# A room of 768 KB for the SyncE transfers of a gated-scan attention and FFN kernel

## The chip, the core and the metric

One core of a Trainium2 chip runs the whole kernel in one launch. The metric is the device time of that launch in microseconds (us), taken over several runs. The core has five engines with a queue of their own each: TensorE (PE; its weight loads are PEld), VectorE (DVE), ScalarE (ACT), GpSimd (POOL) and SyncE (SP). SP does no arithmetic here: it issues nearly all the transfers (DMAs), one after the other in the order in which the program wrote them. POOL issues the rest.

## The reference

```python
def _attn_ref(q, k, v, a_re, a_im):          # each (4, 8, 768, 48)
    mag = np.sqrt(a_re * a_re + a_im * a_im)
    scale = np.minimum(mag, 0.999) / (mag + 1e-06)
    a_re_n, a_im_n = (a_re * scale, a_im * scale)
    for t in range(S):
        ar, ai = (a_re_n[:, :, t, :, None], a_im_n[:, :, t, :, None])
        new_re = ar * S_re - ai * S_im
        new_im = ar * S_im + ai * S_re
        kv = np.einsum('bhd,bhe->bhde', k[:, :, t], v[:, :, t])
        S_re, S_im = (new_re + kv, new_im)
        y[:, :, t] = np.einsum('bhd,bhde->bhe', q[:, :, t], S_re)
    return y

def _moe_ref(x, w1, w2, w3, w_out):          # x is (3072, 384): y with its heads beside each other
    a = x @ w1                               # w1, w2: (384, 1024)
    b = x @ w2
    h = a * b @ w3                           # w3: (1024, 1024)
    return h @ w_out                         # w_out: (1024, 384)
```

## The kernel before, in words

**Units.** The 4 batches of 768 time steps are cut into 8 units of 384 steps (`u` = 0 to 7, two to a batch; `TT` = 384), and a unit into three chunks of 128. For each unit, DVE and ACT turn the gates `a_re` and `a_im` into running products of magnitude and running sums of angle and multiply them into `q` and `k` (`gates`, L574, a generator of some thirty steps). SP moves the results from one layout of the on-chip memory to another as the tiles `KL` and `QL` (12 transfers a unit, `move`, L733). PE then transposes (`turn`, "tr"), builds the state (`state`, "kv"), the scores (`scores`, "sc", which read `KL` and `QL`) and the outputs (`outputs`, "y"), and ACT copies the outputs to `xT` (L815). The FFN of a unit runs on PE while the next unit's attention is fed in between: `ffn_ab` (L844) makes `a * b` (products at L852, ACT copies one at L857, DVE multiplies at L859), `ffn_out` and `out_pair` multiply by the product of `w3` and `w_out`, which was made once at the start (`fuse`, L1140).

**Weights.** `w1` and `w2` arrive as 64-bit words and are rounded to 32 bits on DVE and ACT, in four blocks of 256 columns, `n` = 0 to 3 (`w12_ops`, L1108, and `weight_ops`, L980: DVE at L992, L1006 and L1009, ACT at L997). `fetch` (L962) loads a block: one transfer for the part of `w1` and one for that of `w2`, 768 KB each, into one `raw` tile. There are two `raw` tiles, so block 2 may be loaded when block 0 is rounded, block 3 when block 1 is.

**The order on SP.** From the start of the planned part on (`paced` is filled there) the program order is SP's order. Around the change it is: the rest of block 0; V of unit 0 (`turn_v`, 14 transfers of 18 to 72 KB); block 1; block 2; V of unit 1; block 3; `k`, `q` (three transfers of 192 KB each) and `vr` (576 KB) of unit 1; `re` and `im` of unit 2; the moves of unit 1; outputs. Later units repeat: V, `re`, `im`, the 12 moves, `k`, `q`, outputs and `vr`. `im` of unit u+1 goes into the buffer that unit u's cosine used, so it waits for DVE's L719; `re` waits for the end of the angle sums (L687, L690).

**What SP waits for already.** A transfer waits for the buffer that it fills and for the data that it reads. Each transfer uses one of eight completion counters in turn, so it waits too for the transfer eight places before it. Two single holds are written by hand: the part of `w2` of block 1 waits for the DVE copy of unit 0's second half of the scores of chunk 1 (`pending`, `behind`, L532), and `k`, `q` and `vr` of unit 4 (`LATER`) are issued only at the end of unit 3, behind ACT's last copy of its outputs.

**The planner.** `run` (L1268) decides on the host, with a simple clock, between which PE pieces the gate steps are written; for the first pieces a fixed `PLAN` does. Beside that, POOL reads every weight and part of the gates once more and tests their range (`check_weights`, the tile `look`, 256 KB at a time by its own DMA queue).

Of the kernel before, what the change touches and what calls it, by code (L numbers as in the profile page):

```python
# [376 lines left out]
def kernel(  # L377
# [36 lines left out]
    nc = tc.nc  # L414
    B, H, D, S = qt.shape
    P = 128
# [16 lines left out]
    LO, HI = 32, D - 32  # L433
    PASS, WIDE, SCAN, LAND, SLACK, LATE, RING, LOOK, NEAR, EARLY = 1.17, 1.4, 1.05, 1.8, 0.7, 1.2, 8, 4.0, 4, 2
    LOOKS = 3
    LATER = (4,)
    PLAN = ("- uc c cu c uu - cu uu cuuuc - - cc - - uc uu u - uuucu ucuu u u cuccc uccuucuu - - uu uucc uuc u "
            "uuucu cc ccc ccc cc ccc - - - c - - - - - - c - - c c c cc - cc - ccc - c - cc cc - cc ccc ccc - c c "
            "cccc - - - o - - ").split()
# [53 lines left out]
    st_ang = singles.tile([P, NU, KD, UC], FP, name="st_ang")  # L493

    g_t, L_t, xT_t, ab_t, T_t, KT_t = {}, {}, {}, {}, {}, {}

    clock = dict(PE=0.0, ACT=0.0, DVE=0.0, POOL=0.0, SP=0.0, DMA=0.0)
    ready, landings = {}, [0.0] * RING
# [7 lines left out]
            landings.append(clock["DMA"])  # L506
        ready[name] = clock["DMA"] + 0.2

    def load_rows(dst, src, u, which=range(KD), queue=nc.sync, key=None):
        b, h = divmod(u, 2)  # L510
        for i, f in enumerate(which):
            ins = queue.dma_start(out=dst[:, i, 0:TT], in_=src[b, :, DG * f:DG * (f + 1), h * TT:(h + 1) * TT].rearrange(  # L512
                "h d s -> d h s"))
            if key and i == 0:
                behind(ins, key)

    def load_gates(u, names=("re", "im"), after=()):
        g = g_t.setdefault(u, {})
# [8 lines left out]
        g["q"] = gate_pool[u % 2].tile([P, KD, TT], FP, tag="q", name="q")  # L527
        g["k"] = gate_pool[u % 2].tile([P, KD, TT + 1], FP, tag="k", name="k")

    last = {}  # L530

    def behind(ins, key):  # L532
        if key in last:
            tc.add_manual_dep(ins.ins, last[key].ins.name, BEHIND, reason="room")

    def load_qkv(u, key=None):
        b, h = divmod(u, 2)
        if "q" not in g_t.get(u, {}):
            take_qk(u)
        g = g_t[u]  # L540
        load_rows(g["k"], kt, u, key=key)
        load_rows(g["q"], qt, u)
        landed(("q", u))

    def load_v(u):
        b, h = divmod(u, 2)


        vr = one.tile([P, UC, DM], FP, tag="vr", name="vr")
        nc.sync.dma_start(out=vr, in_=v[b, h * TT:(h + 1) * TT].rearrange("(c p) e -> p c e", p=C))  # L550
        g_t[u]["vr"] = vr

    def turn_v(u):
        b, h = divmod(u, 2)
        src = v[b, h * TT:(h + 1) * TT].rearrange("(c p) (h d) -> p c h d", p=C, d=D)
        for hd in range(H):
            r = SB * (hd % LANES)
            for p0, p1, s0 in ((r, C, 0), (0, r, C - r)):
                if p1 > p0:
                    nc.sync.dma_start(out=Vb[u % 2][p0:p1, :, hd, 0:D], in_=src[s0:s0 + p1 - p0, :, hd])  # L560

    def check_gates(u, re, junk, x):
        scale, bias = ((-1.0, LEAST), (1.0, MOST))[x]
        nc.scalar.activation(out=junk, in_=re, func=AF.Relu, scale=scale, bias=bias, accum_out=st_low[:, x, u, 0:1])

    chained, paced = [], []

    def chain(ins):

# [4 lines left out]
    def gates(u, split):  # L574
# [158 lines left out]
        def move(dst, src, s):  # L733
            for x in range(2):
                for f in range(KD)[s]:
                    nc.sync.dma_start(out=dst[x * KD + f::2 * KD], in_=src[x][:, f])

        for s in [slice(f, f + 1) for f in range(KD)] if split else parts:
            if split:
# [5 lines left out]
                tt(out=q[:, s], in0=q[:, s], in1=Z[:, s], op=OP.mult)  # L745
            move(QL, (A, q), s)
        landed("moves", ("ks", "qs"), 4 * KD, 0.95)
        if 2 < u + 1 < NU and u + 1 not in LATER:
            load_qkv(u + 1)
        yield None  # L750

# [19 lines left out]
    def scores(u, c, x):  # L771
        QL, KL = L_t[u][0:2]
        w = slice(c * C, (c + 1) * C)
        A = Ab[(u * UC + c) % 2]
        n = H // 2
        sc = Sc[x]
        for s0 in SPANS:
            for j in range(n):
                g = (s0 // SB + j) % LANES
                nc.tensor.matmul(out=sc[SB * g:SB * g + SB, j, s0:C], lhsT=KL[:, x * n + j, w][:, s0:s0 + SB],  # L780
                                 rhs=QL[:, x * n + j, w][:, s0:C], start=True, stop=True)
        with tc.high_priority():
            last["sc", u, c, x] = nc.vector.copy_predicated(out=A[:, x * n:(x + 1) * n], data=sc, mask=mask)  # L783


    SPANS = (0, 3 * SB, SB, 2 * SB)
# [7 lines left out]
    def outputs(u, c):  # L794
        QL = L_t[u][0]
        w = slice(c * C, (c + 1) * C)
        A, V = Ab[(u * UC + c) % 2], Vb[u % 2][:, c]
        if c == 0:
            xT_t[u] = two.tile([P, KD, TT], FP, tag="xT", name="xT")
        T = T_t.get((u // 2, u % 2 * UC + c))  # L800
        first = T is None
        y = ps_v.tile([P, KD, C], FP, tag="v", name="y")
        lanes = [[] for _ in range(4)]
        for i, q in enumerate(QUADS):
            f, j = divmod(i, 4)
            o = y[32 * j:32 * j + 32, f]
            got = [(part(V, hd, e), A[:, hd]) for hd, e in q]
            if not first:
                got += [(part(T, hd, e), QL[:, hd, w]) for hd, e in q]
            lanes[j] += [(o, a, b, n == 0, n == len(got) - 1) for n, (a, b) in enumerate(got)]  # L810
        for step in zip(*lanes):
            for o, a, b, s0, s1 in step:
                nc.tensor.matmul(out=o, lhsT=a, rhs=b, start=s0, stop=s1)  # L813
        with tc.high_priority():
            last["y", u, c] = nc.scalar.copy(out=xT_t[u][:, :, w], in_=y)  # L815

    Tb = [singles.tile([2 * D, H, 64], FP, name=f"T{i}") for i in range(3)]
    for T in Tb:
# [2 lines left out]
    def state(u, c):  # L821

        KT, V = KT_t.pop((u, c)), g_t[u]["vr"][:, c].rearrange("p (h d) -> p h d", d=D)
        n = u % 2 * UC + c
        T = T_t.get((u // 2, n))
        kv = ps_v.tile([2 * D, H, D], FP, tag="v", name="kv")
        for hd in range(H):
            rows = KT[:, hd].rearrange("p d x f -> p (d x f)")
            for g in range(0, 2 * D, SB):
                nc.tensor.matmul(out=kv[g:g + SB, hd], lhsT=rows[:, g:g + SB], rhs=V[:, hd], start=True, stop=True)  # L830
        Tn = Tb[(u * UC + c) % 3]
        with tc.high_priority():
            if T is None:
                nc.scalar.copy(out=Tn[:, :, 0:D], in_=kv)
            else:
                nc.vector.tensor_tensor(out=Tn[:, :, 0:D], in0=kv, in1=T[:, :, 0:D], op=OP.add)
        if c == UC - 1:
            rho = L_t[u][1][:, :, TT:TT + 1].to_broadcast([2 * D, H, D])
            nc.vector.tensor_tensor(out=Tn[:, :, 0:D], in0=Tn[:, :, 0:D], in1=rho, op=OP.mult)
        T_t[u // 2, n + 1] = Tn  # L840
        if 1 < u + 1 < NU and u + 1 not in LATER and c == UC - 1 - u % 2:
            load_v(u + 1)

    def ffn_ab(u, j):  # L844
# [40 lines left out]
    def out_pair(u):  # L885
# [5 lines left out]
        def done(t, half):  # L891
            r0 = u * TT + t * P
            if u == NU - 1:
                s = slice(half * DH, (half + 1) * DH)
            elif half == 0:
                return
            else:
                s = slice(0, DM)
            nc.sync.dma_start(out=out[r0:r0 + P, s], in_=o[t][:, s])

        def product(p, bank, i):
            if i == 0:
# [32 lines left out]
    def ffn_out(u, t, parts=1):  # L935
        got = {}

        def part(f0):
            if f0 == 0:
                got["m"] = ps_m.tile([P, DM], FP, tag="mm", name="o")  # L940
            m = got["m"]
            for f in range(f0, f0 + KF // parts):
                nc.tensor.matmul(out=m, lhsT=ab_t[u][:, f, t * P:(t + 1) * P], rhs=w3o[:, f],  # L943
                                 start=(f == 0), stop=(f == KF - 1))
            if f == KF - 1:
                o = (late[0] if u else two).tile([P, DM], FP, tag="o", name="ot")
                nc.scalar.copy(out=o, in_=m)
                r0 = u * TT + t * P
                nc.sync.dma_start(out=out[r0:r0 + P, :], in_=o)
        return [lambda i=i: part(i * KF // parts) for i in range(parts)]  # L950


# [4 lines left out]

    cv = {}

    pending = []  # L960

    def fetch(srcs, early=None, wait=None):  # L962

        if srcs[0].dtype == FP:
            return srcs
# [3 lines left out]
        for src in srcs:  # L969
            r, m = src.shape[1:]  # L970
            t = raw[:, n:n + r * m].rearrange("p (r m) -> p r m", r=r)
            if wait and got:
                pending.append(lambda t=t, src=src: behind(nc.sync.dma_start(out=t, in_=src), wait))
            else:
                nc.sync.dma_start(out=t, in_=src)
            got.append(t.rearrange("p r (m w) -> p r m w", w=2))
            n += r * m
# [100 lines left out]
    def columns(src, j0, j1):  # L1078
        n = 1 if src.dtype == FP else 2
        return words(src)[:, :, n * j0:n * j1]  # L1080
# [3 lines left out]
    def w12_load(n, parts=slice(0, KD), early=()):  # L1084
# [9 lines left out]
                got.setdefault(n, []).append((parts, k, raw.rearrange("p r (m w) -> p r m w", w=2)))  # L1094
        if not early:
            got.setdefault(n, []).extend((parts, k, t) for k, t in enumerate(
                fetch([columns(w, n * WB, (n + 1) * WB)[:, parts] for w in (w1, w2)],
                      wait=("sc", 0, 1, 1) if n == 1 else None)))
        landed(("raw", n), (), 2, 2.2)

    def w12_early():
# [166 lines left out]
    def run(seq):  # L1268
# [82 lines left out]
        for k, (kind, f) in enumerate(seq):  # L1351
# [11 lines left out]
                held.update(tr=[], kv=0)  # L1363
            elif kind == "end":
                ended[0] = f
                if f + 1 in LATER:
                    load_qkv(f + 1, ("y", f, UC - 1))
                    load_v(f + 1)
                if f == 1:
                    load_qkv(2)  # L1370
                    turn_v(2)
# [7 lines left out]
            else:  # L1379
                if kind == "sc":  # L1380
                    clock["PE"] = max(clock["PE"], ready["moves"])
                if kind == "y0" and pending:
                    pending.pop()()
                item(kind)
                f()
                if k >= len(PLAN):
# [114 lines left out]
```

## Time and profile before

| | us |
|---|---|
| runs | 549.95, 549.74, 546.41 (median 549.74) |
| the profiled execution | 552.84 |
| its span, first to last instruction | 551.0 |
| PE busy in the span | 519.4 |
| POOL busy / DVE busy | 361.6 / 359.9 |
| SP's DMA queue busy | 48.1% of the 16 engines' span |

All transfers land on 16 DMA engines. The median times from issue to landing, with the size of one transfer, from the page's last part:

```profile
look<-in_w_dram POOLq DMA_DIRECT2D x56, 256.0 KB, 3.8
...
KL<-gR SPq DMA_DIRECT2D x24, 192.5 KB, 5.3
KL<-k SPq DMA_DIRECT2D x24, 192.5 KB, 6.0
...
k<-in_k_dram SPq DMA_DIRECT2D x24, 192.0 KB, 7.6
q<-in_q_dram SPq DMA_DIRECT2D x24, 192.0 KB, 7.3
...
raw<-in_w_dram SPq DMA_DIRECT2D x6, 768.0 KB, 5.1
```

How to read the lines that follow in this document. A timeline line holds the start, the busy time, the engine, the line of the program, the operation, what it writes and reads, how often, and in brackets how long its engine sat idle before it and what ended that. A line of SP says when a transfer was issued, not when it landed; times of landing are from the trace's record of each transfer's completion. A line of windows holds the stretch, its length, the busy time of PE, PEld, DVE, ACT and POOL, the clock granted to PE (1.00 is full), the share of the DMA engines' time, and GB/s.

### The profile page before, as it was taken

The numbers are of one execution on the slowest core, as the hardware profiler recorded it, in microseconds if no ns is written. First come the engines' busy times: TensorE is split into PE (matmuls) and PEld (weight loads), VectorE is DVE, ScalarE is ACT, GpSimd is POOL, SyncE is SP. The second block draws the span as 40 slices with busy tenths as digits, with TensorE's granted clock in tenths as the row PEclk, the third lists the DMA queues.
The fourth block names the chain that finished last, engine by engine and source line by source line (L and its number), as shares of the span: only waits on it lengthen the run. The fifth ranks groups of instructions, "written<-read, shape, count | busy, mean of one in ns | idle before, by whom it ended". The sixth has DMA issues, their size and how long they took to land.

```text
span 551.0 us, 13249 instructions
## 1 busy us (share of the span) xinstructions
PE 519.4 (94%) x5474; PEld 357.7 (65%) x5474; DVE 359.9 (65%) x520; ACT 273.7 (50%) x391; POOL 361.6 (66%) x425
## 2 busy tenths in 40 slices
PE   4789799989999999999998999999999999999995
PEld 2345475547656885669664875678567956696574
DVE  7999598856586669675956788597448851331131
ACT  6988866636544464754374626934276323101100
POOL 1000000488888888888998899899899988888000
PEclk9899999999999999999999999999999999999998
DMA  8999677594669835592889348933792182223001
GB/s 269 358 404 271 159 238 186 167 213 139 158 171 225 230 98 152 130 216 67 230 191 239 112 123 181 228 104 115 172 243 81 56 225 67 74 81 87 0 3 49
DMA packets 73222, 89.73 MB, mean 163 GB/s; under 512 B 31808, under 2 KB 62976, under 8 KB 72384
## 3 DMA queue, kind: packets, MB, share of 16 engines
q1 hardware_dynamic: 67072, 69.78, 48.1%
q0 software_dynamic: 6080, 19.01, 12.1%
q8 instruction: 45, 0.74, 0.6%
q14 instruction: 25, 0.20, 0.1%
HBM read 65.14 MB, written 4.72 MB: 127 GB/s over the span
## 4 chain that ended last, share of the span: by engine, by line
PE 74%; DVE 7%; DMA 7%; ACT 4%; SPq 4%; issue 3%; DVEq 0%; ACTq 0%
PE m L852 34%; PE p L907 12%; PE o L943 9%; PE y L813 6%; PE sc L780 5%; DMA im<-in_a_im_dram 3%; PE kv L830 3%; PE f L1145 2%; SPq L512 2%; PE tp L766 2%; DMA raw<-in_w_dram 1%; DMA q<-in_q_dram 1%; PE sc L1145 1%; ACT gZ L586 1%; DMA out_dram<-ot 1%
## 5 line engine op out<-in xcount | busy, mean ns | idle before, releaser
L852 PE MATMUL m<-xT,w1s 128*128 128x384 f32 x384 | 134.8, 487 | 1.2 <-ACT xT L815 1.2
L852 PE MATMUL m<-xT,w2s 128*128 128x384 f32 x384 | 135.1, 488 | 0.0
L852 PEld LDWEIGHTS m<-xT,w1s 128*128 128x128 f32 x384 | 72.2, 190 | 48.9 <-ACT xT L815 1.7
L852 PEld LDWEIGHTS m<-xT,w2s 128*128 128x128 f32 x384 | 71.5, 190 | 46.2
L1064 POOL TENSOR_SCALAR look<-look 128x256 f32<-128x256 f32 (+1 forms) x84 | 88.3, 1052 | 7.3
L859 DVE TENSOR_TENSOR ab<-m,a 128x384 f32<-128x384 f32 x64 | 35.2, 553 | 72.1 <-PE m L852 67.1
L1045 POOL TENSOR_TENSOR seen<-seen,look 128x256 bf16<-128x256 bf16 (+1 forms) x84 | 77.1, 918 | 6.8
L857 ACT COPY a<-m 128x384 f32<-128x384 f32 x64 | 30.2, 472 | 100.8 <-PE m L852 100.8
L1029 POOL MEMSET seen<- 128x256 bf16 x1 | 0.3, 311 | 98.9 <-DVE w2s L1009 98.9
L943 PE MATMUL o<-w3o,ab 128*128 128x384 f32 x160 | 54.3, 489 | 2.3 <-DVE ab L859 2.3
L1061 POOL TENSOR_TENSOR look<-look 128x256 f32<-128x256 f32 (+1 forms) x72 | 52.8, 733 | 3.0 <-DMA look<-in_w_dram 1.2
L1063 POOL TENSOR_SCALAR look<-look 128x256 f32<-128x256 f32 (+1 forms) x44 | 48.4, 1101 | 4.9 <-DMA look<-in_a_re_dram 1.7
L1066 POOL TENSOR_TENSOR look<-look 128x256 f32<-128x256 f32 (+1 forms) x44 | 42.9, 975 | 3.7
L1040 POOL DMA_DIRECT2D look<-in_w_dram x56 | 33.1, 591 | 16.6 <-POOL seen L1045 16.6
L943 PEld LDWEIGHTS o<-w3o,ab 128*128 128x128 f32 x160 | 29.7, 190 | 21.9 <-DVE ab L859 2.9
L783 DVE COPY_PREDICATED A<-mask,sc 128x512 f32<-128x512 uint8 x48 | 32.7, 734 | 12.9 <-PE sc L780 12.9
L813 PE MATMUL y<-A,V 128*32 128x128 f32 x768 | 39.4, 273 | 0.0
L768 ACT COPY KT<-tp 128x384 f32<-128x384 f32 x40 | 34.2, 863 | 6.4 <-PE tp L766 6.4
L813 PE MATMUL y<-QL,T 96*32 96x128 f32 x640 | 34.9, 272 | 0.8 <-issue 0.8
L813 PEld LDWEIGHTS y<-A,V 128*32 128x32 f32 x768 | 34.2, 110 | 1.6 <-issue 1.6
L815 ACT COPY xT<-y 128x384 f32<-128x384 f32 x24 | 11.4, 476 | 47.4 <-PE y L813 47.4
L1145 PE MATMUL f<-wo_s,w3s 128*128 128x384 f32 x96 | 34.6, 509 | 0.0
(123 smaller groups left out, 892.8 us busy)
## 6 DMA issues: line engine op xcount, KB each, us to landing
look<-in_w_dram POOLq DMA_DIRECT2D x56, 256.0 KB, 3.8
raw<-in_w_dram SPq DMA_DIRECT2D x6, 1024.0 KB, 10.3
KL<-gR SPq DMA_DIRECT2D x24, 192.5 KB, 5.3
KL<-k SPq DMA_DIRECT2D x24, 192.5 KB, 6.0
re<-in_a_re_dram SPq DMA_DIRECT2D x24, 192.0 KB, 3.9
im<-in_a_im_dram SPq DMA_DIRECT2D x24, 192.0 KB, 4.3
k<-in_k_dram SPq DMA_DIRECT2D x24, 192.0 KB, 7.6
q<-in_q_dram SPq DMA_DIRECT2D x24, 192.0 KB, 7.3
```

Of the source, the lines that this page charges most:

```text
L768: nc.scalar.copy(out=KT_t[u, c][:, :, :, x].rearrange("p h d f -> p f d h"), in_=tp.rearrange("p f (d h) -> p f d h", h=H))
L813: nc.tensor.matmul(out=o, lhsT=a, rhs=b, start=s0, stop=s1)
L852: nc.tensor.matmul(out=m, lhsT=w[:, j * P // WB, f, j * P % WB:j * P % WB + P], rhs=xT_t[u][:, f], start=(f == 0), stop=(f == KD - 1))
L859: nc.vector.tensor_tensor(out=ab_t[u][:, j], in0=m, in1=got[0], op=OP.mult)
L907: nc.tensor.matmul(out=m[p], lhsT=a[:, f], rhs=b[:, f], start=(f == 0), stop=(f == KH - 1))
L943: nc.tensor.matmul(out=m, lhsT=ab_t[u][:, f, t * P:(t + 1) * P], rhs=w3o[:, f], start=(f == 0), stop=(f == KF - 1))
L1045: nc.gpsimd.tensor_tensor(out=seen[:, 0:n], in0=seen[:, 0:n], in1=x, op=OP.add)
L1061: tt(out=x, in0=x, in1=x, op=OP.mult)
L1063: ts(out=y, in0=x, scalar1=high, scalar2=None, op0=OP.is_le)
L1064: ts(out=x, in0=x, scalar1=low, scalar2=None, op0=OP.is_ge)
L1066: tt(out=x, in0=x, in1=y, op=OP.mult)
L1145: nc.tensor.matmul(out=sums[j], lhsT=w3_t[f][:, j * P:(j + 1) * P], rhs=w3_t["wo"][:, f], start=(f == 0), stop=(f == KF - 1))
```

## The change

A list `flights` keeps the size of every transfer that SP issues from the planned part on. A new transfer adds up sizes backwards, itself first; at the first older transfer with which the sum passes `ROOM` (768 KB), it is made to wait until that one has landed. `w1` and `w2` go out by row (256 KB, three to a part), so that they fit. Both single holds go; `k`, `q` and `vr` of unit 4 then take the place that they have in the other units. All of SP's transfers of the planned part go through `transfer`; POOL's do not.

```diff
-    LATER = (4,)
+    ROOM = 4 * 192 * 1024
...
+    paced, flights = [], []
+
+    def transfer(dst, src):
+
+        ins = nc.sync.dma_start(out=dst, in_=src)
+        if paced:
+            size = total = 4 * math.prod(dst.shape)
+            for other, n in reversed(flights):
+                total += n
+                if total > ROOM:
+                    tc.add_manual_dep(ins.ins, other.ins.name, BEHIND, reason="room")
+                    break
+            flights.append((ins, size))
...
-    def load_rows(dst, src, u, which=range(KD), queue=nc.sync, key=None):
+    def load_rows(dst, src, u):
         b, h = divmod(u, 2)
-        for i, f in enumerate(which):
-            ins = queue.dma_start(out=dst[:, i, 0:TT], in_=src[b, :, DG * f:DG * (f + 1), h * TT:(h + 1) * TT].rearrange(
-                "h d s -> d h s"))
-            if key and i == 0:
-                behind(ins, key)
+        for f in range(KD):
+            transfer(dst[:, f, 0:TT], src[b, :, DG * f:DG * (f + 1), h * TT:(h + 1) * TT].rearrange("h d s -> d h s"))
...
-                    nc.sync.dma_start(out=Vb[u % 2][p0:p1, :, hd, 0:D], in_=src[s0:s0 + p1 - p0, :, hd])
+                    transfer(Vb[u % 2][p0:p1, :, hd, 0:D], src[s0:s0 + p1 - p0, :, hd])
...
-                    nc.sync.dma_start(out=dst[x * KD + f::2 * KD], in_=src[x][:, f])
+                    transfer(dst[x * KD + f::2 * KD], src[x][:, f])
...
-        if 2 < u + 1 < NU and u + 1 not in LATER:
+        if 2 < u + 1 < NU:
             load_qkv(u + 1)
...
-            if wait and got:
-                pending.append(lambda t=t, src=src: behind(nc.sync.dma_start(out=t, in_=src), wait))
-            else:
+            for i in range(r) if paced else ():
+                transfer(t[:, i], src[:, i])
+            if not paced:
                 nc.sync.dma_start(out=t, in_=src)
...
-                if f + 1 in LATER:
-                    load_qkv(f + 1, ("y", f, UC - 1))
-                    load_v(f + 1)
...
-                if kind == "y0" and pending:
-                    pending.pop()()
```

The loads of `vr` and the stores of the outputs call `transfer` in the same way.

## The prediction

> **What bounds the kernel now.** I read the page first, then the windows, then the timelines of PE, DVE and SP around PE's waits. The page's busy line and its chain:
>
> ```profile
> PE 519.4 (94%) x5474; PEld 357.7 (65%) x5474; DVE 359.9 (65%) x520; ACT 273.7 (50%) x391; POOL 361.6 (66%) x425
> ...
> PE 74%; DVE 7%; DMA 7%; ACT 4%; SPq 4%; issue 3%; DVEq 0%; ACTq 0%
> ```
>
> TensorE works through nearly the whole span, so only what opens or closes one of its gaps counts. The windows (start:end, length, busy time of each engine, granted clock, DMA share, GB/s) show where gaps are left; PE is full from 80 to 100 and is not in the other two rows:
>
> ```profile
> 80.00:100.00 20.00, 20.00 (x64) 11.79 (x63) 17.76 (x27) 12.71 (x15) 0.00 (x0) 1.00 0.81 229
> 100.00:120.00 20.00, 17.70 (x62) 10.50 (x61) 15.03 (x15) 11.26 (x17) 14.89 (x18) 1.00 0.64 164
> ...
> 280.00:300.00 20.00, 17.29 (x152) 10.85 (x151) 10.59 (x13) 13.53 (x17) 17.73 (x20) 1.00 1.02 219
> ```
>
> Of the time in which the change acts (from 69 us on), PE lacks 2.3 us before 120, 2.7 at 294, 1.06 at 245 and some 1.4 around 140. PE's timeline names the first:
>
> ```profile
> 117.55 0.91 PE L943 MATMUL o<-w3o,ab 128*128 128x384 f32 x2 [2.30 <-DVE ab L859]
> ```
>
> VectorE's timeline shows why that product came late:
>
> ```profile
> 94.33 0.56 DVE L992 TENSOR_SCALAR low<-raw 128x768 int32<-128x768 int32 x1 [1.62 <-DMA raw<-in_w_dram]
> ...
> 99.58 1.38 DVE L654 TENSOR_TENSOR k<-k,gR 128x1152 f32<-128x1152 f32 x1
> ...
> 102.19 1.37 DVE L656 TENSOR_TENSOR q<-q,gA 128x1152 f32<-128x1152 f32 x1
> ...
> 115.58 1.46 DVE L600 TENSOR_TENSOR im<-im,gR 128x1152 f32<-128x1152 f32 x1 [1.64 <-DMA im<-in_a_im_dram]
> 116.95 0.54 DVE L859 TENSOR_TENSOR ab<-m,a 128x384 f32<-128x384 f32 x1
> ```
>
> DVE waits for weight block 3 at 94.33, then runs unit 1's gate steps (k, q, then L702, ACT's cosine, L717, L719). L719 frees the buffer into which SP loads unit 2's `im`; L600 waits for that, and the product that PE needs stands behind L600. From 94.33 to 117.55 there is no slack. SP's timeline shows what feeds it:
>
> ```profile
> 69.24 0.41 SPq L975 DMA_DIRECT2D raw<-in_w_dram  x1
> 73.83 0.38 SPq L973 DMA_DIRECT2D raw<-in_w_dram  x1
> 76.72 0.90 SPq L975 DMA_DIRECT2D raw<-in_w_dram  x2
> 77.67 11.27 SPq L560 DMA_DIRECT2D V<-in_v_dram  x14
> 89.05 0.93 SPq L975 DMA_DIRECT2D raw<-in_w_dram  x2
> 90.03 1.96 SPq L512 DMA_DIRECT2D k<-in_k_dram  x3
> 92.03 2.05 SPq L512 DMA_DIRECT2D q<-in_q_dram  x3
> ```
>
> Block 1 (first two lines, the second held), block 2, V of unit 1, block 3, then k and q of unit 1, in one queue.
>
> **The change, part by part.** PE, DVE, ACT and POOL keep their instructions and order; only SP's list differs. On SP, 6 transfers of 768 KB become 18 of 256 KB, and k, q of unit 4 move ahead of one output. Twelve more issues at 0.45 us (a 256 KB row took 0.43 to 0.55) are 5.4 us, hidden inside waits that SP now has anyway.
>
> *The hold on block 1's w2 goes.* It landed at 78.69 and DVE used it at 80.64: 2 us of cover, so worth nothing.
>
> *The new wait, blocks 2 and 3.* Three rows of 256 KB fill the room, so each row waits for the one three back. A lone row's landing is not in the trace. Bounds: 2.9 us (POOL's 256 KB look, alone, around 255) and 3.8 us (the two 256 KB rows at 58.4, behind the moves). Nearest by size: 192 KB alone took 3.0 and 768 KB alone 4.9, so 3.0 + 64/576 x 1.9 = 3.2, which I take. Data spacing follows the same slope, 0.82 per row.
> - Block 2 starts at 76.72 as before (its buffer). Rows land at 79.92, 80.74, 81.56; the next three go at 79.97, 80.79, 81.61 and land at 83.17, 83.99, 84.81.
> - Queued behind: V of unit 1. Its first piece fits only when block 2's fourth row is down, 83.2 instead of 77.67. Before, V stuck for 2.7 us in its middle on block 2's landing (85.1), which now goes. Fourteen pieces took 8.05 to 8.9 us in other units; 8.5 ends V at 91.7 instead of 88.94.
> - Block 3's first two rows go at 91.75 and 92.2, the third when the last V piece is down (91.3 + 2.1 = 93.4), landing at 96.6 against 94.31: DVE's wait grows by 2.3. The other rows go at 95.0, 95.8, 96.65 and land at 98.2, 99.0, 99.85.
> - k's third transfer waits for the last row: issued 99.9, landed 102.9. DVE would want it at 99.58 + 2.3 = 101.9; it gets it at 102.95, which is 3.4 late. q lands at 105.1, wanted at 105.5, no more cost.
>
> With no slack on to 117.55, PE loses 3.4 us. With 2.9 per row and 8.05 for V the same steps give 1.6; with 3.8 and 8.9 they give 6.1. Range 1.6 to 6.1.
>
> The Trainium skill, page "DMA: Bandwidth & Descriptors", sections "Anatomy of one DMA" and "Bandwidth", advises batching to at least 1 MiB because each DMA has about 2.0 us of fixed time beside bytes/436e3 us, which speaks against the split. By its formula a 256 KB row takes an estimated 2.6 us and the same steps give 0.9; for 768 KB it gives 3.8 where this trace has 4.9, so I go by the trace.
>
> *The moves of KL and QL.* With a KL of 192.5 KB in the sum only three fit, among QL four. In the stretch 282 to 302 they land 0.9 to 1.1 us apart, bounded by the DMA engines; three in flight at 2.9 us (a KL alone at 442.6) give one per 0.98. So nothing to 0.2 us per unit, and PE needs QL only 4.4 us or more later in units 1, 2, 4 to 7. In unit 3 there is no cover: QL's last part landed at 245.65, the scores began at 245.96 after PE's 1.06 us gap. There I take +0.4, between -1.06 (gap gone) and +0.9 (one look of 256 KB more in front).
>
> *k, q of unit 4, no longer held.* They land around 250 instead of 269.7. DVE used them at 269.71 and 271.45 without a DMA wait, so nothing is gained. They now run beneath unit 3's scores and outputs; where k, q of unit 2 did so (136 to 144), PE had gaps of 0.78 (released by nothing the profile shows) and 0.58 (ACT's copy). Cost 0 to 1.4; I take 0, because the second is ACT's and four transfers in flight are fewer than the eight of that time.
>
> *SP held longer.* Outputs, `vr` and `re` stand behind the waits for up to 4 us. `re` of unit 2 waits for `vr`'s landing and is down near 113; ACT wants it at 110.1 + 3.4 = 113.5: hidden, barely. V of units 2 and 3 shifts by 2 us, `re` of unit 3 still comes before its `im` may go.
>
> Sum: 3.4 + 0.4 = 3.8 us. On the profiled execution, 552.84 us (span 551.0), 556.6; that execution was 3.1 above the median of the runs, so on the median 549.74 + 3.8 = 553.5, or 0.7%. About 1% (5.5 us) is what a measurement of this kernel tells from no change.
>
> **Rivals.**
> *Faster: a shallower queue lets what is urgent through.* Place: unit 5's `im` (280.2), whose third part took 7.0 us against 3.5 at 111.9, with a look and twelve moves close by; DVE waited 4.58 us and PE 2.71. If it comes in time, and the gaps at 245 and 140 close, that is 2.71 + 1.06 + 0.78 = 4.55; less the smallest start cost 1.6, 546.8. It is past 1% only if the start costs nothing either and a little else closes. For: looks took 7.7 us amid the moves, 2.9 alone. Against: `im` goes ahead of the moves in SP's order, and landings keep that order. The same page's section "Queues, rings and completion order" says that an engine takes its queues in turn, which would spare the looks that backlog; the 7.7 speaks otherwise.
>
> *Slower by more.* One mechanism: rows that land in 3.8 us, so that each wait in the chain block 2, V, block 3, k is paid in full: 6.1. With it unit 3 pays its 0.9 and 1.4: 549.7 + 8.4 = 558.1. It decides from a row time of about 3.6.
>
> *The wait changes nothing.* If rows land in 2.6 or less and V issues at its own pace, block 3 is within 1 us of before: 549 to 551. The issue of eight unlanded transfers was bounded before, too; but that was 1.5 MB, so the new wait does bind.
>
> **How the numbers follow.** Forecast (start late by 1.6 to 5, own range 551 to 556): 0.47, of it 0.11 above +1%. Slower rival 0.25. Faster rival 0.19, of it 0.10 beyond 1%. No change 0.09. So faster 0.10, slower 0.36, within 0.54. The range from 547.5 to 558 leaves out about 2 in 10.
>
> **What would show it.** Right: in the new profile V of unit 1 starts near 83, block 3 near 91.7; L992's wait near 94 grows to about 4 us, L654 waits for k, and PE's gap at L943 is near 5.7. Wrong: that gap is 2.3 or less, or a gap of over 2 us opens after 130 that is not in this profile (then I have overlooked whom SP's waits hold up), or the gap at 294 closes.

## The result, and the profile after

| | before | after |
|---|---|---|
| median of the runs, us | 549.85 | 556.42 |
| lowest to highest | 546.41 to 550.15 (4 runs) | 554.57 to 557.47 (4 runs) |
| the profiled execution | 552.84 | 557.29 |
| its span | 551.0 | 555.4 |
| PE idle, unit 0's first state product to unit 1's first scores | 4.4 | 7.4 |
| time lost there to half clock | 0 | 3.4 |

The ratio of the times is 1.0134, with a 95% interval from 1.0093 to 1.0175: slower by 1.3%. The ratios in this document leave out runs more than 1.5% above the fastest run of their kernel: none of the changed kernel's, four of the twelve of "V behind k, q, vr", one of twelve in three other kernels, and two to four of the 23 to 29 of before.

The time is inside the range and 2.9 us above the figure forecast. It is 0.4 us above the 551 to 556 that the prediction gave to its own mechanism; the range reached 558 for the sake of the slower rival. Of the chances, 0.36 stood on a loss of over 1%, and 0.54 on less than 1% either way.

The last two rows are made from the trace's records of PE's products and of the clock (a record of 6.83 us at half clock loses 3.41 us). They are used all through what follows, since that stretch ("the way" from here on) is the same PE work in every kernel here: its length less idle time less lost clock is 61.9 to 63.5 us in every profile (with the products added in one of them taken off). It was 67.3 us long before and 74.1 after. From unit 1's first scores to the last product it was 415.3 and 414.7: in this pair of profiles the loss lies in the start part. For the later units one pair says little. Four other profiles of kernels whose later transfers go out in the order of before gave 410.1, 411.9, 412.9 and 414.6 there, and the second profile of the changed kernel gave 417.0, so the 415.3 of before is long for its kind.

All line numbers are some 2 to 4 higher than before, and all of SP's transfers now have the line of `transfer`, L500. SP's timeline of the profile after:

```profile
68.70 13.62 SPq L500 DMA_DIRECT2D raw<-in_w_dram  x12
83.23 7.79 SPq L500 DMA_DIRECT2D V<-in_v_dram  x14
91.13 4.98 SPq L500 DMA_DIRECT2D raw<-in_w_dram  x6
97.66 1.99 SPq L500 DMA_DIRECT2D k<-in_k_dram  x3
```

The first line holds blocks 1 and 2 (block 2 begins at 77.15). V of unit 1 starts at 83.23 (77.67 before), block 3 at 91.13 (89.05), k at 97.66 (90.03). DVE's timeline shows who waits for it:

```profile
95.85 0.56 DVE L994 TENSOR_SCALAR low<-raw 128x768 int32<-128x768 int32 x1 [3.63 <-DMA raw<-in_w_dram]
...
102.31 1.36 DVE L658 TENSOR_TENSOR k<-k,gR 128x1152 f32<-128x1152 f32 x1 [1.13 <-DMA k<-in_k_dram]
...
118.40 1.36 DVE L604 TENSOR_TENSOR im<-im,gR 128x1152 f32<-128x1152 f32 x1 [1.67 <-DMA im<-in_a_im_dram]
119.68 0.55 DVE L863 TENSOR_TENSOR ab<-m,a 128x384 f32<-128x384 f32 x1
```

The wait for block 3 grew from 1.62 to 3.63, one for k is new, the one for `im` is as before and only later. The products that need L863's result, on PE's timeline:

```profile
116.79 0.91 PE L947 MATMUL o<-w3o,ab 128*128 128x384 f32 x2 [0.68 <-DVE ab L863]
120.28 1.01 PE L947 MATMUL o<-w3o,ab 128*128 128x384 f32 x1 [2.58 <-DVE ab L863]
```

The product at 120.28 took 1.01 us where 0.49 is usual. The windows (columns as before) say why:

```profile
115.92:119.33 3.41, 1.10 (x3) 0.30 (x2) 1.74 (x3) 0.46 (x1) 2.92 (x5) 1.00 0.72 199
119.33:126.16 6.83, 5.88 (x13) 3.69 (x14) 2.17 (x4) 1.99 (x3) 6.09 (x8) 0.50 0.80 224
```

After 3.41 us in which PE was busy for 1.10, the clock granted to it fell to one half, for 6.83 us. Nothing like it came behind the 2.30 us gap before, and the prediction has no term for it. The stretch at 280 shows the one place that looks like a gain (whether it is one is taken up behind the experiments):

```profile
280.00:300.00 20.00, 20.00 (x116) 12.32 (x115) 14.29 (x15) 14.85 (x18) 18.11 (x18) 1.00 0.57 164
```

PE is full there; the 2.71 us gap at 294 is gone.

### The profile page after: what moved, and what is told of

Read it like the earlier page. It is cut to its first block, busy times and chain, and to the rows that moved or that the text cites. A ratio compares the mean times of both kernels' runs of the same rounds, so it can differ in the third digit from the quotient of the medians.

```text
span 555.4 us, 13288 instructions
## 1 busy us (share of the span) xinstructions
PE 523.8 (94%) x5474; PEld 360.0 (65%) x5474; DVE 362.0 (65%) x520; ACT 273.6 (49%) x391; POOL 360.5 (65%) x425
## 4 chain that ended last, share of the span: by engine, by line
PE 68%; DMA 15%; DVE 7%; issue 3%; ACT 3%; SPq 3%; DVEq 0%; ACTq 0%
PE m L856 32%; PE p L911 11%; PE y L817 6%; PE o L947 6%; PE sc L784 5%; DMA raw<-in_w_dram 4%; PE f L1146 3%; DMA im<-in_a_im_dram 3%; SPq L500 2%; PE kv L834 2%; PE tp L770 2%; DMA KL<-gR 2%; PE sc L1146 2%; DMA KL<-k 1%; DMA k<-in_k_dram 1%
## 5 line engine op out<-in xcount | busy, mean ns | idle before, releaser
L1066 POOL TENSOR_SCALAR look<-look 128x256 f32<-128x256 f32 (+1 forms) x84 | 93.9, 1118 | 7.3
L863 DVE TENSOR_TENSOR ab<-m,a 128x384 f32<-128x384 f32 x64 | 35.2, 552 | 74.7 <-PE m L856 69.0
L947 PE MATMUL o<-w3o,ab 128*128 128x384 f32 x160 | 57.0, 506 | 3.8 <-DVE ab L863 3.3
L1063 POOL TENSOR_TENSOR look<-look 128x256 f32<-128x256 f32 (+1 forms) x72 | 53.4, 742 | 1.9
L1065 POOL TENSOR_SCALAR look<-look 128x256 f32<-128x256 f32 (+1 forms) x44 | 46.3, 1053 | 5.6 <-DMA look<-in_a_re_dram 2.4
L1068 POOL TENSOR_TENSOR look<-look 128x256 f32<-128x256 f32 (+1 forms) x44 | 37.4, 851 | 3.7
L784 PE MATMUL sc<-QL,KL 96*32 96x32 f32 (+3 forms) x1536 | 32.4, 236 | 2.7 <-DMA k<-in_k_dram 2.0
```

What stands on the lines that cost most here:

```text
L863: nc.vector.tensor_tensor(out=ab_t[u][:, j], in0=m, in1=got[0], op=OP.mult)
L1063: tt(out=x, in0=x, in1=x, op=OP.mult)
L1065: ts(out=y, in0=x, scalar1=high, scalar2=None, op0=OP.is_le)
L1066: ts(out=x, in0=x, scalar1=low, scalar2=None, op0=OP.is_ge)
L1068: tt(out=x, in0=x, in1=y, op=OP.mult)
```

## The experiments

The theory was: the wait holds V, block 3 and k back; DVE and then PE are late by that; and the longer gap brings the clock down. The rivals were that the rows cost by themselves, that the waits cost all over the later units, and that four runs had misled. "Way" is the stretch defined above; each profile is one execution, the ratios are over 6 or 12 runs and the runs of before taken beside them. The last column is the part of the lost clock that falls near 60 us. The change acts from 69 us on, so this part is not its doing: the profile of before and the first of the changed kernel have none, eleven of the other twelve have 1.7 or 3.4 us. It also gives loads more time to land, so the ways can be compared only roughly. With it taken off, the kernels with 768 KB in the start part and V in its old place have 69.9 to 74.1 us, those with twice that room 67.2 and 67.8, before 67.3, and before with rows 70.7.

| | ratio to before, 95% interval | way, us | idle + lost clock | of it near 60 us |
|---|---|---|---|---|
| the change again | 1.0126, 1.0064 to 1.0188 | 74.1 | 6.0 + 5.1 | 3.4 |
| room in later units only | 1.0016, 0.9979 to 1.0052 | 68.9 | 2.9 + 3.4 | 3.4 |
| room in the start part only | 1.0109, 1.0057 to 1.0161 | 74.7 | 6.1 + 5.1 | 3.4 |
| twice the room | 1.0138, 1.0078 to 1.0198 | 71.2 | 5.1 + 3.4 | 3.4 |
| twice the room, start part only | 1.0033, 1.0001 to 1.0066 | 70.6 | 4.6 + 3.4 | 3.4 |
| before with rows | 1.0007, 0.9965 to 1.0050 | 70.7 | 5.9 + 1.7 | 0 |
| V behind k, q, vr | 1.0032, 0.9983 to 1.0081 | 67.8 | 3.5 + 1.7 | 1.7 |
| V behind re of unit 2 | 1.0075, 1.0036 to 1.0113 | 71.1 | 4.1 + 5.1 | 3.4 |
| before, V behind re of unit 2 | 1.0023, 0.9989 to 1.0057 | 69.9 | 4.0 + 3.4 | 3.4 |
| products put into the gap | 1.0110, 1.0065 to 1.0154 | 71.6 | 3.1 + 1.7 | 1.7 |
| unit 4 held again | 1.0204, 1.0127 to 1.0281 | 73.0 | 6.5 + 3.4 | 1.7 |
| before without holds | 1.0040, 1.0004 to 1.0077 | 69.0 | 2.9 + 3.4 | 3.4 |

### The change again

No edit.

> The changed kernel once more, unedited, as the control of the three runs beside it and of the products put into the gap. Theory A (the loss is block 3 and k landing late in the start part, and one or two windows of half clock behind the longer gap): 1.010 - 1.016 of before, about 6 us more, the way from the first state product of unit 0 to the first scores of unit 1 is 71 - 75 us against 67.3 in before, and from there to the last product within 1 us of before's 415.3. Rival (the 1.013 of the first comparison was the scatter of four runs): within 0.5% of before.

1.0126: the loss is real. The way is 74.1 us again, but for another reason in part: here the gap was 2.61 us with one window of half clock (1.7 us lost) behind it, and 6.83 us of half clock had come at 60. Without the latter it is 70.7 us, 3.4 more than before. From unit 1's first scores to the last product it took 417.0, 1.6 longer than before, a little more than expected; there a gap of 3.06 us in front of unit 3's scores brought 6.83 us of half clock.

### Where the loss lies

The room and the rows only behind the start part (`loose` is filled when vr of unit 1 has been issued):

```diff
-        if paced:
+        if loose:
...
-            for i in range(r) if paced else ():
-                transfer(t[:, i], src[:, i])
-            if not paced:
-                nc.sync.dma_start(out=t, in_=src)
+            nc.sync.dma_start(out=t, in_=src)
...
+                loose.append(True)
```

> The changed kernel with the room and the rows taken out of the start part: blocks of w1 and w2 whole and unheld, transfers wait for room only from re of unit 2 on. Theory A (the loss lies in the start part alone): V of unit 1 starts near 77.7 again, VectorE's wait for block 3 near 94 is 1.6 again, the way from unit 0's first state product to unit 1's scores 67 - 69 us, time within 0.3% of before. Rival (the waits of units 2 to 7 cost by themselves, the clock drop at 252 among them): 1.004 - 1.010 of before with the start part as before.

1.0016. The waits of all later units, unit 4 unheld, cost nothing that these runs can measure; the interval leaves room for 2.9 us. V of unit 1 went out at 80.94 and not near 77.7, and DVE's wait for block 3 was 0.1 us and not 1.6 (PE, and DVE with it, were later after 6.83 us of half clock at 63).

The other half, the room only in the start part, and unit 4 held as before:

```diff
+    LATER, last, loose = (4,), {}, []
...
-        if paced:
+        if paced and not loose:
...
+                loose.append(True)
```

> The changed kernel with its room and rows in the start part alone (up to vr of unit 1); behind that the transfers go out as in before, k, q and vr of unit 4 held behind unit 3's outputs. It is the complement of the run that had the room in the later units alone (1.0016). Theory A (the loss lies in the start part): 1.010 - 1.016 of before, the way from unit 0's first state product to unit 1's scores 71 - 75 us, SyncE's transfers of unit 3 close together again. Rival (start and later units share the loss, or it needs both): 1.003 - 1.008.

1.0109, the way 74.7: all of the loss that can be measured is in the start part. The rival, that both parts share it, is not borne out, though the two intervals (from 1.0057 here, up to 1.0052 for the later units) do not exclude a share of some tenths of a percent.

### Is it the size of the wait?

```diff
-    ROOM = 4 * 192 * 1024
+    ROOM = 8 * 192 * 1024
```

> The changed kernel with a room of 1536 KB, twice as much; rows as in the change. Theory A (V and block 3 are late because SyncE waits for landings, so the lateness goes with the room): V of unit 1 starts near 80 (83.2 in the change, 77.7 before), VectorE's wait for block 3 falls from 3.6 to 1.5 - 2.2, the wait for k goes, the way from unit 0's first state product to unit 1's scores falls from 74 to 68 - 70, time 1.000 - 1.006 of before. Rival (the rows are what is late, not the wait): wait for block 3 over 3 us, time over 1.009.

The profile moved as expected: V of unit 1 at 80.44, the wait for block 3 1.82 us, none for k. The time did not: 1.0138. With the same room in the start part alone, the question was put again:

> The run before it with a room of 1536 KB. It asks what the changed kernel with twice the room left open: there VectorE's wait for block 3 fell from 3.4 to 1.8 us and that for k went, but the time stayed at 1.0138. Theory A (time follows that wait): 1.000 - 1.006. Theory B (any wait of SyncE in the start part costs this, whatever its size, since rows and V share the engines): 1.010 - 1.016. Theory C (twice the room hurt in the later units, where transfers crowd unit 3's and unit 5's moves): 1.000 - 1.006 here too, with the later part of unit 1's scores to the last product at 415 us.

1.0033 against 1.0109 with 768 KB: in the start part the loss goes with the size of the wait. The two intervals overlap a little (up to 1.0066 and from 1.0057), but the two kernels ran beside each other and can be compared directly: their runs average 551.2 us (547.5 to 553.9) and 555.9 (553.0 to 558.1). Theory B's 1.010 lies outside this interval. DVE's timeline of this run:

```profile
95.29 0.56 DVE L998 TENSOR_SCALAR low<-raw 128x768 int32<-128x768 int32 x1 [0.64 <-DMA raw<-in_w_dram]
101.31 1.36 DVE L662 TENSOR_TENSOR k<-k,gR 128x1152 f32<-128x1152 f32 x1 [0.69 <-DMA k<-in_k_dram]
```

The two waits are 1.33 us together, where the changed kernel has 4.76. That leaves the 1.0138 to the later units with 1536 KB and unit 4 unheld. From unit 1's scores on, its profile has 415.3 us where this one has 410.1, with gaps of 1.12, 0.92 and 2.20 us at 246, 252 and 296 that this one has not. But the profile of before has 415.3 too, with this one's order of transfers, so one profile each does not tell why: that stays open.

### Is it the rows?

The rows alone, in the kernel before, all issued at once and the holds kept:

```diff
+            def rows(t=t, src=src):
+                return [nc.sync.dma_start(out=t[:, i], in_=src[:, i]) for i in range(r)]
...
+            elif paced:
+                rows()
```

> The kernel before with one part of the change alone: w1 and w2 of each block go out as three rows of 256 KB, all issued at once, the two holds kept, no room. Theory A (rows by themselves cost nothing; it is the wait between them that holds V and block 3 back): time within 1 us of before (549.8), block 3's last rows land within 1 us of before's 96.64, no half clock near 119. Rival (the split itself costs, more and smaller transfers that share the engines): block 3 lands over 1 us later, the TensorE gap at 117.5 grows past 2.5, time 552 - 556.

1.0007: over the runs, rows cost nothing that can be measured (up to 2.7 us by the interval). V started at 79.17, block 3 at 89.12, and DVE waited 1.29 us for it. In the profile DVE then waited 0.22 us for the rest of block 3, 0.63 for k (not at all before) and 2.18 for `im` (1.64 before), and the gap was 3.04 us with half clock behind it, against what was expected. The twelve runs were level with before all the same: one profile of this kernel says less than its runs.

### What is behind the wait: V

In the changed kernel, V of unit 1 behind block 3, k, q and vr:

```diff
                 load_qkv(1)
                 load_v(1)
+                turn_v(1)
+                landed("V", (), 14, 0.3, 0.57)
...
-                if f + 1 < NU and f != 1:
+                if 1 < f + 1 < NU and f != 1:
```

> The changed kernel with one edit: the fourteen V transfers of unit 1 are issued behind block 3, k, q and vr of unit 1 instead of in front of them; only SyncE's order differs. Theory A (the loss of the start part comes from block 3 and k landing late behind V, and the longer TensorE gap then halves the granted clock): VectorE's wait of 3.63 us for block 3 (near 95.8) and its 1.13 us for k fall under 0.3, the TensorE gap of 2.58 us in front of the last two w3o products of the first half falls under 1, no half clock near 119, and the time falls from 556.4 by about 2.3 + 2.9 to 550 - 552. Rival (the loss is spread over later units, because each SyncE transfer waits): those waits go, but the time stays within 1.5 us of 556.4. Second rival (V or re of unit 2 become late): a new wait of over 1 us of the outputs of unit 1 (near 140) or of ScalarE's first Ln of unit 2, and no gain.

1.0032. Its SP timeline:

```profile
71.74 16.27 SPq L500 DMA_DIRECT2D raw<-in_w_dram  x15
89.52 2.31 SPq L500 DMA_DIRECT2D k<-in_k_dram  x3
91.87 2.37 SPq L500 DMA_DIRECT2D q<-in_q_dram  x3
95.95 0.39 SPq L500 DMA_DIRECT2D vr<-in_v_dram  x1
97.06 8.64 SPq L500 DMA_DIRECT2D V<-in_v_dram  x14
105.81 1.84 SPq L500 DMA_DIRECT2D re<-in_a_re_dram  x3
107.82 2.54 SPq L500 DMA_DIRECT2D im<-in_a_im_dram  x3
```

The rows still wait for each other, yet block 3 and k are down before DVE wants them: its waits for them are gone, and `im` of unit 2, which follows DVE's L723, goes out at 107.82 instead of 113.29. The gap was 2.13 us, not under 1: DVE's wait for `im` (3.13 us) now ended with ACT's work on `re`, which stood behind V. So the second rival had its part in it; but by the ratio most of the loss went with the place of V. This kernel's runs scatter most (547.9 to 562.3 us) and the median of all twelve is 1.006 of before's, so the gain is less sure than the ratio makes it look. A next place, behind `re`:

```diff
             load_gates(u + 1, ("re",), ("ang",))
+            if u == 1:
+                turn_v(1)
...
-                    turn_v(f + 1)
+                    if f:
+                        turn_v(f + 1)
```

> The changed kernel with V of unit 1 behind re of unit 2, so that it lies neither in front of block 3 nor in front of k or re; SyncE stands idle there for 8 us. With V in front of re of unit 2 the loss fell from 1.013 to 1.003, but im of unit 2 then had ScalarE's work on the late re in front of it and a gap of 2.13 us. Theory A: re of unit 2 lands by 104 and im by 112, the gap falls under 1, no half clock near 119, time 0.998 - 1.004 of before. Rival (im of unit 2 waits behind V's 8 us of issue): im goes out after 111, gap over 2, time 1.003 - 1.010.

1.0075, as the rival had it. SP's and DVE's timelines of this run:

```profile
103.81 8.02 SPq L500 DMA_DIRECT2D V<-in_v_dram  x14
111.94 1.84 SPq L500 DMA_DIRECT2D im<-in_a_im_dram  x3
```

```profile
117.00 1.38 DVE L604 TENSOR_TENSOR im<-im,gR 128x1152 f32<-128x1152 f32 x1 [4.13 <-DMA im<-in_a_im_dram]
```

`re` goes out from 98.97 to 103.8, for its parts wait for room, so V's 8 us of issue end at 111.9 and not before `im` may go. The wait moved from block 3 to `im`. The same edit in the kernel before, where SP is done with `re` at 98.74:

> The kernel before with one edit: the V transfers of unit 1 go out behind re of unit 2, into the 12 us in which SyncE stands before im of unit 2. Theory A, turned the other way (the start part is set by block 3's landing, then im of unit 2, then the gap in front of the last products of w3o): block 3 goes out near 78 and lands by 88, VectorE's 1.62 us before it goes, im of unit 2 goes out 1.5 - 3 us earlier, the 2.30 us gap near 117 falls under 1, time 0.995 - 0.998 of before. Rival (the gap has another bound right behind, ScalarE's work on re of unit 2): VectorE's wait goes but the gap stays over 1.8 and time is within 0.2%. Second rival (V comes too late for the outputs of unit 1 or im of unit 2 waits behind V): a new wait near 140 or at im, time above before.

DVE's wait for block 3 went and the gap too (0.34 us is left in front of the last two products of `w3o`), but the time is 1.0023: no gain. `im` of unit 2 went out at 110.72, not earlier than before's 110.70. In the profile 3.41 us were lost to half clock at 60, which slows PE until the transfers have caught up and so may hide what the edit gains; whether it is so in the other eleven runs is open.

### The clock

Six products into the gap of the changed kernel, their results unused:

```diff
+                for _ in range(6 if (u, t, f) == (0, 0, KF - 2) else 0):
+                    nc.tensor.matmul(out=Sc[1].rearrange("p l c -> p (l c)")[:, 0:DM], lhsT=ab_t[u][:, 0, 0:P], rhs=w3o[:, 0],
+                                     start=True, stop=True)
```

> The changed kernel with six products of 128x384 more on TensorE, whose results are not used (they go to a scores bank that is free then), in the middle of the 2.58 us gap near 118; nothing of the computation is left out. Theory A (the idle stretch is what halves the granted clock from 119.33 to 126.16): the gap's end stays where it is, the clock stays whole there, the products behind it take 0.32 us each and not 0.64, and the time falls by 2.5 - 3, to 553.5. Rival 1 (the clock fell for another reason, such as load over a longer time): half clock at the same place, time within 0.5 us of 556.4. Rival 2 (the half clock is there but the work behind it has slack): the clock stays whole and the time stays at 556.4.

PE's timeline:

```profile
117.50 4.03 PE L948 MATMUL sc<-w3o,ab 128*128 128x384 f32 x12
121.38 1.45 PE L950 MATMUL o<-w3o,ab 128*128 128x384 f32 x4
```

Each product is two records, so they filled 3.9 us; the gap's end is at 121.38 with a start 1.3 us later than in the changed kernel's first profile, so it stayed about where it was. The clock stayed whole from 67 to 251 and four records took 1.45 us. The way is 2.5 us shorter than 74.1, as theory A had it, though 1.7 us were lost near 60 here. But the time, 1.0110, cannot be told from 1.0126 or 1.0134. In the profile no half clock follows once the gap is filled, as theory A says of the idle stretch; what that is worth over the runs is not shown.

### The holds

The hold of unit 4 put back in the changed kernel:

```diff
+    LATER, last = (4,), {}
...
+                if f + 1 in LATER:
+                    load_qkv(f + 1, ("y", f, UC - 1))
+                    load_v(f + 1)
```

> The changed kernel with the hold of before on k, q and vr of unit 4 put back (they go out behind the last outputs of unit 3). Theory A (unheld k and q of unit 4 lie in front of unit 3's moves on the queue or on the DMA engines, so QL lands 0.8 us later against im(4), the TensorE gap there grows from 1.06 to 1.99 and the clock halves from 252.45 to 255.9): gap near 1.1, no half clock near 252, time lower by 0.9 + 1.7, about 553.8. Rival 1 (the longer gap comes from SyncE's spacing of the moves themselves): gap stays at 1.9 - 2.0, half clock stays, time within 0.5 us of 556.4. Rival 2 (the held k, q of unit 4 come late for unit 4's VectorE work): a wait for k of unit 4 near 300, time up by 1 - 2.

The theory fell: the gap in front of unit 3's scores was 3.26 us, not 1.1, with half clock, and the time rose to 1.0204. The new cost is later. SP's timeline, and PE's:

```profile
267.86 2.47 SPq L501 DMA_DIRECT2D k<-in_k_dram  x3
...
290.70 2.37 SPq L501 DMA_DIRECT2D im<-in_a_im_dram  x3
```

```profile
297.80 1.11 PE L838 MATMUL kv<-vr,KT 128*32 128x48 f32 x48 [3.51 <-ACT KT L776]
```

Held until 267.86, k, q, vr and V then go out by the room, and `im` of unit 5 follows at 290.70, where the changed kernel has 287.40; PE waits 3.51 us and loses a window of clock. So taking the hold away seems to belong to the room, though the interval, from 1.0127, overlaps that of the changed kernel.

The kernel before without its two holds:

```diff
-    LATER = (4,)
+    LATER = ()
...
-                      wait=("sc", 0, 1, 1) if n == 1 else None)))
+                      wait=None)))
```

> The kernel before with its two holds taken out and nothing else: w2 of block 1 goes out at once, k, q, vr of unit 4 right behind unit 3's moves. Theory A (the holds are worth nothing, since the later units of the changed kernel cost nothing either): 0.998 - 1.003 of before, unit 3's gap in front of its scores 1.0 - 2.7 us. Rival (k and q of unit 4 crowd the last QL parts of unit 3): QL lands over 1 us later against im of unit 4, gap over 2.7 with half clock behind it, time 1.003 - 1.008. Other side (re and im of unit 5 come earlier): the gap of 2.71 us near 294 goes, time 0.995 - 0.998.

1.0040: the time is the rival's, while the gap is theory A's. QL's last part landed 19.6 us after `im` of unit 4 was issued, 0.7 later than before, unit 3's gap was 2.03, and one of 2.31 us opened at its outputs. Without a room, the two holds together are worth some 2 us (0.2 to 4.2 by the interval); with 768 KB of room the later units cost nothing measurable without them.

## Why the prediction was right, and where it was short

- **SP's times.** V at 83.2, block 3 from 91.75 with its last row down at 99.85, k at 102.9, q at 105.1 were forecast; 83.23, 91.13, 99.02, 102.19 and 104.88 came. Rows took 2.9 to 3.6 us in blocks 2 and 3, against 3.2 taken. That the times agree so closely is in part luck. The execution was 1.27 us ahead of before at unit 0's first state product (60.46 against 61.73), and "Block 2 starts at 76.72 as before (its buffer)" does not hold. Its buffer is free when DVE has read block 0 for the last time. DVE's timeline before, where block 2 went out at 76.72:

```profile
76.34 0.31 DVE L1006 TENSOR_SCALAR w2s<-raw 128x256 int32<-128x256 int32 x1
```

and after, where it went out only at 77.15:

```profile
75.07 0.28 DVE L1008 TENSOR_SCALAR w2s<-raw 128x256 int32<-128x256 int32 x1
```

There it waited for a row of block 1, issued at 72.42 and down at 77.00: the room held block 2 as well, for some 1.7 us, and no term has that. V's issue, 7.8 us for 8.5 taken, gave a part of it back. The chain block 2, V, block 3, k was right, and V's place in it, the runs with V moved and with the room changed in the start part alone bear out.
- **Lateness on DVE.** Counted from unit 0's first state product, L994 started 2.8 us later than before and L658 4.0, for 2.3 and 3.4.
- **PE's gap.** One gap of 5.7 us was expected. It came as four (0.83, 0.51, 0.68 and 2.58 us), since earlier `ab` products wait for DVE too. In all PE's idle time in the stretch grew by 2.9 us, for 3.4, and by 1.6 in the second profile, where PE had been slowed near 60: the term was right within its 1.6 to 6.1.
- **A term that is missing is the clock.** "With no slack on to 117.55, PE loses 3.4 us" counts idle time only. The idle time brought 3.4 us of lost clock with it in the first profile and 1.7 behind the gap in the second. Over the runs the mean granted clock was 0.985 in the ten runs of the changed kernel and 0.987 to 0.989 in the runs of before beside the experiments, an estimated 1.1 to 2.2 us in 553. The forecast was 2.9 us short, and the clock may be a good part of that; it is not shown, for the run with the gap filled was no faster.
- **Unit 3.** +0.4 with 0.9 as the upper end; +0.93 came, with 1.7 of lost clock. PE's timeline before and after:

```profile
245.96 1.32 PE L780 MATMUL sc<-QL,KL 96*32 96x128 f32 x64 [1.06 <-issue]
```

```profile
251.67 1.70 PE L784 MATMUL sc<-QL,KL 96*32 96x128 f32 x64 [1.99 <-DMA k<-in_k_dram]
```

The second profile of the changed kernel has 3.06 there, and "a gap of over 2 us opens after 130 that is not in this profile" was a sign of being wrong. The gap scatters, but not without order: in the seven profiles with 768 KB of room in the later units it is 1.9 to 3.3 us, 2.5 on the mean; in the five with the transfers of before there it is 0 to 1.95, 0.9 on the mean (1.06 in before, 1.95 with the rows). So the room seems to lengthen it by more than the 0.4 taken, some 1.7 by these profiles, which would be another part of what the forecast lacked. The run with the room in later units only (-1.2 to +2.9 us by its interval) neither shows nor excludes it.
- **The formula for rows** that the prediction sets beside its own steps stands in that page for transfers that GpSimd issues, which the prediction does not say. SP's rows in blocks 2 and 3 took 2.9 to 3.6 us, not the estimated 2.6.
- **k, q of unit 4.** "Cost 0 to 1.4; I take 0" holds within this room. Without the room it was low: about 2.2 for both holds together. The hold on block 1's w2 was not tried alone; the run with room in the later units only lacks it too, at 1.0016.
- **The rivals.** The gap at 294 closed, which stood under "wrong" and was the faster rival's place. Kernels whose order of transfers there is that of before had no such gap either (1.04 us with the room at the start alone; under 0.6 with twice that room, with the rows alone, and with V moved in before), so it looks like chance in the one profile of before and not like a gain of the change. The slower rival (3.8 us rows) reached a time near the measured one by another road: rows were not 3.8.
- **`re` of unit 2** was hidden: DVE's wait for ACT's cosine (L721) was 2.11 us before and after.

None of the twelve kernels is faster than before.

## What to carry to other kernels

A limit on what is in flight was paid here by what stood in the queue between two urgent loads: look for the small, unurgent transfers there (fourteen pieces of V, 8 us of issue) and find them a place before the limit is set; which place matters (1.0032 and 1.0075). A gap on TensorE that a change lengthens to some 2 us or more is to be priced with the clock that it may cost, not with its length alone. And gaps of one or two us far from the change, in one profile, are no ground for a rival.

## What the runs showed of the hardware

Within one execution all records of half clock begin on one grid of 3.413 us, and they are one or two windows long, but for the last, which runs past the last product; the grid's place differs from one execution to the next. In the fourteen profiles, behind unit 0, from 100 us on, the next window went with the busy share of PE in the one before it:

```
busy share of the window    windows    half clock in the next
0.14 to 0.36                   9           9
0.41 to 0.48                   8           3
0.52 to 0.58                   7           0
```

So a gap of 2.30 us (before, share 0.41) went unpunished and one of 1.95 us (rows alone, 0.43) did not, and a gap of 2.65 us that fell on two windows (0.56 the lower) cost no clock (V behind k, q, vr). The share is not the whole rule. Near 60 us, around unit 0's first state products, half clock followed all six windows of 0.42 to 0.52 and five of eight of 0.55 to 0.56; why these differ is open.

The Trainium skill, page "TensorE: Matmul & The Clock Gate", section "Part 1: The HAM clock gate (the "warmup" mystery)", says that the window is 3413 ns long and runs freely, which these records bear out. It gives at least one idle window as the condition of half rate; here windows with PE busy for a third of the time were enough (nine of nine of 0.14 to 0.36).
